# Two pads in SBUF that move u, w0, w1, h, k and t to multiples of 64 bytes

## The chip, the cores and the metric

The kernel runs on one core of a Trainium2 chip. The metric is the device time of one execution in microseconds, as the median of several runs. Beside the times there is one profiled execution, from whose trace all rows below come. A second core is not used, so there is no exchange between cores.

## The reference

For 4 batches, 12 heads, 448 tokens and head width 64, the reference computes attention in which the heads are mixed before and after the softmax, and then a feed-forward block:

```python
scores = scale * q @ k^T                        # per head, 448 x 448
scores = einsum('bhij,hg->bgij', scores, w_pre) # mix heads
attn = softmax(scores)
attn = einsum('bhij,hg->bgij', attn, w_post)    # mix heads again
x = (attn @ v), heads side by side              # 4 x 448 x 768
u = x + (x^T @ U @ V)^T                         # rank 32, along the tokens
out = u + relu(u @ w_ch1) @ w_ch2               # 768 -> 3072 -> 768
```

## The kernel before

**Attention.** The work is cut into 16 units of at most 120 tokens. For a unit, `qk` (L381) multiplies q by k in float32, two heads at a time, into PSUM; `qk_out` (L385) copies the scores to a buffer s; `relay` (L388) sends each head's rows of s by DMA into t, where the partitions hold (token, head) pairs. `premix` (L412) multiplies t by the mixing weights, `neg_max` (L417) and `exp` (L422) make the softmax, `postmix` (L447) mixes again and transposes, `post_out` (L455) copies to a buffer a, and `av` (L488, L496) multiplies by v and puts the result in `acc`. Every matmul of this part is in float32; a float32 matmul stands in the trace as two instructions. There are two t buffers, t0 and t1, three q, two k and three s.

**Rank-32 step.** For two of the 768/128 columns at a time, `flip` (L677) transposes acc, `by_u` (L694) multiplies the result (xh and xl, 256 columns wide) by U, and `by_v` (L708) multiplies a buffer t3 by the buffer v4 (448 columns). The last two run in float32r, as the feed-forward block does.

**Feed-forward block.** u and the weights are split in a high and a low float32r part, and each product is made as three matmuls. `up` (L750) streams uh or ul of a batch (128 x 448) past a 128 x 128 block of w0h or w0l: 18 matmuls for one block f of 128 hidden columns and one batch. `down` (L770) streams hh or hl past blocks of w1h or w1l. f runs over 24 blocks and b over 4 batches, so that there are 24 x 4 x 18 = 1,728 matmuls at L750 and as many at L770, 3,456 in all. `relu_h` (L755) and `relu_l` (L759) write hh and hl, `gather` (L773) adds the products to acc, and `store` (L776) writes acc out. Weights arrive in pieces as 64-bit words in a buffer kr (`piece`, L568 to L638). Each piece is narrowed by five steps on VectorE (L596, L600, L601, L605, L606), one on ScalarE (L589) and one on GpSimd (L610), through a pair of buffers x and a, and then written into w0 or w1 (L299, L306). Pieces take turns with their x and a: those of one piece are in the pool tmp1, those of the next in tmp2.

**Order.** A planner lays out the order of all steps from costs and ranks. From f = 2 on the order of the steps on each engine is written out by hand (`lines`, L823 to L846). Neither reads an address.

**Where the buffers lie.** SBUF is filled from two sides. Pools of the left side follow one another upwards from byte 1,152 of each partition, those of the right side downwards from byte 229,344. When a stage ends, its pools are given back and the feed-forward buffers take their place, all from the right. A buffer's size is rounded up to a multiple of 32 bytes. Counted from the sizes in the code, the first bytes before are these, and what remains after division by 64:

| buffer | first byte | remainder |
|---|---|---|
| kr (2) | 222,176 and 225,760 | 32 |
| tmp1 | 219,104 | 32 |
| tmp2 | 44,416 | 0 |
| k (2), later u of batch 0 | 197,600 and 208,352 | 32 |
| q (3) | 188,672, 191,648, 194,624 | 0, 32, 0 |
| s (3) | 177,920, 181,504, 185,088 | 0 |
| u of batch 1, 2, 3 | 176,096, 148,448, 80,864 | 32 |
| w0 (2) | 169,952 and 120,800 | 32 |
| w1 (3) | 102,368, 108,512, 114,656 | 32 |
| h (12 of 1,792 bytes) | from 126,944 | 32 |
| t0, t1 | 148,256, 126,752 | 32 |
| xh, xl, t3, u4, v4 | 47,488, 51,584, 55,680, 57,216, 59,264 | 0 |
| v, a1, a0, e (3) | 61,056, 73,344, 93,504, from 114,176 | 0 |

The rows inside these buffers are 1,792 bytes (k, t, u, h, s) or 3,072 bytes (w0, w1), multiples of 64, so that every row of a buffer has the remainder of its first byte. The rows of a are 480 bytes: even rows have remainder 0, odd rows 32. In `av` the two heads of a pair read an even and an odd row beside each other.

Of the kernel before, what the change touches and what calls it, by code (L numbers as in the profile page):

```python
# [8 lines left out]
F32 = mybir.dt.float32  # L9
F32R = mybir.dt.float32r  # L10
I32 = mybir.dt.int32
# [7 lines left out]
B, H, S, D = 4, 12, 448, 64  # L19
# [16 lines left out]
HW = DM // 2  # L36
# [45 lines left out]
def f32(ap):  # L82
    return ap.bitcast(F32)
# [159 lines left out]
def build(tc, q2, kt, vj, wpre_in, wpost_in, u_in, v_in, ident, w1j, w2, out, show=None):  # L243
    nc = tc.nc
    whole, tail_ctx, a_ctx, mix_ctx, t1_ctx, t0_ctx, qk_ctx = (ExitStack() for _ in range(7))
    sb = {}

    def pool(ctx, name, bufs, side="left", **kw):
        sb[name] = Pool(ctx.enter_context(tc.tile_pool(name=name, bufs=1, side=side, **kw)), plan.where)
        return sb[name]  # L250
# [17 lines left out]
    p = pool(whole, "c", 1)  # L268
# [6 lines left out]
    pool(mix_ctx, "wc", 1)  # L275
    for n in ("e", "wr", "st"):
        pool(mix_ctx, n, BUFS[n])
    pool(t1_ctx, "t1", 1)
    pool(t0_ctx, "t0", 1)
    for n in ("kr", "tmp1"):  # L280
        pool(whole, n, BUFS[n], "right")
    for n in ("k", "q", "s"):
# [7 lines left out]
    T = {}  # L290
# [166 lines left out]
    for k in range(NC // 2):  # L457
        r = 2 * k
        us = sorted({chunks[2 * k][0], chunks[2 * k + 1][0]})
        pre, post, st, e, wr = ("pre", k), ("post", k), ("st", k), ("e", k), ("wr", k)  # L460
# [107 lines left out]
    def piece(key, src, n, p, rank, finish, slots, opened, cost, early=None, steady=False):  # L568


        count[0] += 1
        which = f"tmp{1 + count[0] % 2}"

        def pair(slot):
            T["nx", key], T["na", key] = (sb[slot[0]].tile([128, HW], I32, e, slot) for e in "xa")

        def get():
            return T["raw", key][:p, :n], T["nx", key][:p, :n], T["na", key][:p, :n]

        def load_raw(eng):  # L580
            T["raw", key] = sb["kr"].tile([128, 2 * S], F32, "kr", raw)[:, :2 * HW].bitcast(I32).rearrange("p (n t) -> p n t", t=2)
            eng.dma_start(out=T["raw", key][:p, :n], in_=src)

        def narrow0(eng):
            pair(first_tmp)
            raw, x, a = get()
            top = raw[:, :, 1]
            if eng is nc.scalar:
                eng.activation(out=f32(x), in_=f32(top), func=ACTF.Abs)  # L589
            else:  # L590
                eng.tensor_scalar(out=x, in0=top, scalar1=0x7FFFFFFF, scalar2=None, op0=ALU.bitwise_and)

        def narrow1(eng):
            raw, x, a = get()
            top = raw[:, :, 1]
            eng.tensor_scalar(out=a, in0=top, scalar1=LOW_EXP, scalar2=3, op0=ALU.bitwise_and, op1=ALU.logical_shift_left)  # L596

        def narrow2(eng):
            raw, x, a = get()
            eng.scalar_tensor_tensor(out=a, in0=raw[:, :, 1], scalar=SIGN_TOP, in1=a, op0=ALU.bitwise_and, op1=ALU.bitwise_or)  # L600
            eng.scalar_tensor_tensor(out=f32(a), in0=f32(x), scalar=MIN_NORMAL, in1=f32(a), op0=ALU.is_ge, op1=ALU.mult)  # L601

        def narrow3(eng):
            raw, x, a = get()
            eng.tensor_scalar(out=x, in0=a, scalar1=SIGN_EXP, scalar2=None, op0=ALU.bitwise_and)  # L605
            eng.scalar_tensor_tensor(out=f32(x), in0=raw[:, :, 0].bitcast(U32), scalar=2.0**-52, in1=f32(x), op0=ALU.mult, op1=ALU.mult)  # L606

        def narrow4(eng):
            raw, x, a = get()
            eng.tensor_tensor(out=f32(a), in0=f32(a), in1=f32(x), op=ALU.add)  # L610

        def put(eng):
            T["nf", key] = dram.tile([128, HW], F32, "nf" + "_".join(str(k) for k in key))
            eng.dma_start(out=T["nf", key][:p, :n], in_=f32(get()[2]))

        def take(eng):
            pair(tmp)
            eng.dma_start(out=f32(get()[2]), in_=T["nf", key][:p, :n])

        s = n / HW  # L620
        raw, tmp = ("kr", key), (which, key)
        kept = early is not None and len(early) == 2
        first_tmp = ("tmp1", (key, "early")) if early else tmp
        r0 = early[1] if early else rank
        plan.add((key, 0), [("SP", (480, 1800 * s))], load_raw, r0 - RANK["raw"], [early[0] if early else opened], [raw])
        plan.add((key, "abs"), [("ACT", 60 + 395 * s), ("DVE", 60 + 210 * s)][:1 if steady else 2], narrow0, r0, [(key, 0)], [raw, first_tmp])
        plan.add((key, 1), [("DVE", 60 + 212 * s)], narrow1, r0, [(key, "abs")], [raw, first_tmp])
        plan.add((key, 2), [("DVE", 120 + 1000 * s)], narrow2, r0, [(key, 1)], [raw, first_tmp], port=("DVE",))
        plan.add((key, 3), [("DVE", 120 + 750 * s)], narrow3, r0, [(key, 2)], [raw, first_tmp], port=("DVE",))
        plan.add((key, 4), [("POOL", 100 + 900 * s), ("DVE", 60 + 410 * s)][:1 if steady else 2], narrow4, r0, [(key, 3)], [first_tmp], port=BOTH)  # L630
        if kept:
            plan.add((key, "put"), [("SP", (480, 900 * s))], put, r0, [(key, 4)], [first_tmp])
            plan.add((key, "take"), [("SP", (480, 900 * s))], take, rank - RANK["raw"], [(key, "put"), opened], [tmp])
        used = tmp if kept or not early else first_tmp
        if early and not kept:
            rank = r0
        plan.add((key, 5), cost[0], lambda eng: finish(0, eng, f32(get()[2])), rank, [(key, "take" if kept else 4), opened], [used] + slots, port=BOTH)
        plan.add((key, 6), cost[1], lambda eng: finish(1, eng, f32(get()[2])), rank, [(key, 5)], [used] + slots, port=BOTH)  # L638
# [153 lines left out]
    for f in range(KF):  # L792
# [8 lines left out]
        for b in range(B):  # L801
# [9 lines left out]
            n = 1 if (f, b) == (KF - 1, B - 1) else 2  # L811
# [20 lines left out]
    for f in range(RANK["even"], KF):  # L832
        for b in range(B):
            lines["PE"].append(("up", f, b))
            key = ("w", f + 1, b)
# [79 lines left out]
```

## Time and profile before

| | |
|---|---|
| median of 3 runs | 1097.73 us (1089.36 to 1101.10) |
| profiled execution | 1100.28 us |
| its span, first to last instruction | 1098.5 us |
| mean granted TensorE clock | 0.992 |
| TensorE matmul busy | 1059.1 us (96%) |
| VectorE, ScalarE, GpSimd busy | 666.5, 408.4, 271.9 us |

The profiled execution's own time is 1.8 us more than its span. Busy times are sums over the span; matmuls overlap in the records, so the pace of a run of matmuls is read from their starts or from the chain of waits, not from the duration of one. [...]

### The profile page before, as it was taken

The numbers are of one execution on the slowest core, as the hardware profiler recorded it, in microseconds if no ns is written. First come the engines' busy times: TensorE is split into PE (matmuls) and PEld (weight loads), VectorE is DVE, ScalarE is ACT, GpSimd is POOL, SyncE is SP. The second block draws the span as 40 slices with busy tenths as digits, with TensorE's granted clock in tenths as the row PEclk, the third lists the DMA queues.
The fourth block names the chain that finished last, engine by engine and source line by source line (L and its number), as shares of the span: only waits on it lengthen the run. The fifth ranks groups of instructions, "written<-read, shape, count | busy, mean of one in ns | idle before, by whom it ended". The sixth has DMA issues, their size and how long they took to land.

```text
span 1098.5 us, 28397 instructions
## 1 busy us (share of the span) xinstructions
PE 1059.1 (96%) x12120; PEld 874.2 (80%) x12120; DVE 666.5 (61%) x1076; ACT 408.4 (37%) x852; POOL 271.9 (25%) x398
## 2 busy tenths in 40 slices
PE   4798999999999999999999999999999999999998
PEld 1365666665666899999999999999999999999997
DVE  0574564565688687665665666565666566566634
ACT  2786677677768721222112212212221211221200
POOL 3131111111224522232222222222222222222200
PEclk8899999999999999999999999999999999999999
DMA  7665646635755211221122212111211211221105
GB/s 277 191 187 171 196 128 193 200 119 167 213 198 163 82 31 44 58 58 58 44 58 58 58 44 58 56 46 58 58 48 53 58 44 57 58 58 44 44 1 200
DMA packets 52270, 108.11 MB, mean 98 GB/s; under 512 B 5056, under 2 KB 38320, under 8 KB 51632
## 3 DMA queue, kind: packets, MB, share of 16 engines
q1 hardware_dynamic: 52144, 106.30, 31.4%
q8 instruction: 95, 1.56, 0.6%
q14 instruction: 31, 0.25, 0.1%
HBM read 57.91 MB, written 7.08 MB: 59 GB/s over the span
## 4 chain that ended last, share of the span: by engine, by line
PE 89%; DMA 4%; ACT 3%; DVE 2%; issue 2%; SPq 0%; POOL 0%; ACTq 0%; DVEq 0%
PE bank L750 33%; PE bank L770 33%; PE bank L447 6%; PE bank L488 5%; PE bank L381 5%; PE bank L412 5%; DMA t<-s 3%; ACT e L422 2%; PE bank L496 1%; DVE mx L417 1%; PE bank L677 1%; PE bank L694 1%; ACT s L299 1%; DMA k<-in_kt 0%; ACT a L299 0%
## 5 line engine op out<-in xcount | busy, mean ns | idle before, releaser
L773 DVE TENSOR_TENSOR acc<-acc,bank 128x896 f32<-128x896 f32 (+1 forms) x153 | 163.5, 1070 | 173.5 <-PE bank L770 172.9
L755 ACT ACTIVATE hh<-bank 128x448 fp32r<-128x448 f32 x96 | 52.4, 546 | 492.2 <-PE bank L750 312.2
L750 PE MATMUL bank<-uh,w0l 128*128 128x448 f32 x576 | 212.2, 368 | 0.0
L770 PE MATMUL bank<-hh,w1l 128*128 128x448 f32 x576 | 212.1, 368 | 0.0
L770 PE MATMUL bank<-hl,w1h 128*128 128x448 f32 x576 | 211.9, 368 | 0.0
L770 PE MATMUL bank<-hh,w1h 128*128 128x448 f32 x576 | 211.9, 368 | 0.0
L750 PE MATMUL bank<-uh,w0h 128*128 128x448 f32 x576 | 211.9, 368 | 0.0
L750 PE MATMUL bank<-ul,w0h 128*128 128x448 f32 x576 | 211.9, 368 | 0.0
L610 POOL TENSOR_TENSOR a<-a,x 128x384 f32<-128x384 f32 (+2 forms) x98 | 98.6, 1006 | 422.6 <-PE bank L750 381.2
L417 DVE TENSOR_REDUCE mx<-bank 128x2 f32<-128x896 f32 x90 | 97.7, 1088 | 69.5 <-PE bank L412 63.7
L447 PEld LDWEIGHTS bank<-wr,e 60*64 60x64 f32 x5040 | 89.4, 135 | 45.8 <-issue 31.9
L422 ACT ACTIVATE e<-bank,mx 128x448 f32<-128x448 f32 x180 | 113.3, 642 | 13.0 <-DVE mx L417 9.2
L770 PEld LDWEIGHTS bank<-hh,w1l 128*128 128x128 f32 x576 | 108.1, 188 | 11.1 <-DVE acc L773 0.3
L770 PEld LDWEIGHTS bank<-hh,w1h 128*128 128x128 f32 x576 | 108.1, 188 | 10.9
L750 PEld LDWEIGHTS bank<-uh,w0l 128*128 128x128 f32 x576 | 108.1, 188 | 10.9
L750 PEld LDWEIGHTS bank<-uh,w0h 128*128 128x128 f32 x576 | 108.1, 188 | 10.9
L770 PEld LDWEIGHTS bank<-hl,w1h 128*128 128x128 f32 x576 | 108.1, 188 | 10.8
L750 PEld LDWEIGHTS bank<-ul,w0h 128*128 128x128 f32 x576 | 108.1, 188 | 10.8
L381 PE MATMUL bank<-k,q 64*64 64x448 f32 (+1 forms) x768 | 96.1, 569 | 15.5 <-ACT s L299 9.0
L759 DVE SCALAR_TENSOR_TENSOR hl<-bank,hh 128x448 fp32r<-128x448 f32 x96 | 59.9, 624 | 81.3 <-ACT hh L755 81.3
L447 PE MATMUL bank<-wr,e 60*64 60x60 f32 x5040 | 93.3, 219 | 8.9 <-issue 6.6
L412 PE MATMUL bank<-t,wpre 64*64 64x448 f32 x720 | 87.6, 557 | 8.8 <-DMA t<-s 5.8
(61 smaller groups left out, 1105.1 us busy)
## 6 DMA issues: line engine op xcount, KB each, us to landing
t<-s SPq DMA_DIRECT2D x192, 210.0 KB
kr<-in_w1j SPq DMA_DIRECT2D x48, 384.0 KB
kr<-in_w SPq DMA_DIRECT2D x48, 384.0 KB
v<-in_vj SPq DMA_DIRECT2D x4, 1536.0 KB
q<-in_q SPq DMA_DIRECT2D x32, 186.0 KB
out<-acc SPq DMA_DIRECT2D x9, 448.0 KB
k<-in_kt SPq DMA_DIRECT2D x4, 672.0 KB
k<-in_kt SPq DMA_DIRECT2D x4, 448.0 KB
```

The costliest lines, as they stand in the source:

```text
L381: eng.matmul(o[at, i, :S], lhsT=q[d, p, at], rhs=k[d, p, :], start=True, stop=True)
L412: eng.matmul(o[64 * j:64 * j + 64, i, :S], lhsT=wpre[64 * i:min(64 * i + 64, QW)], rhs=tt[u % 2][64 * i:min(64 * i + 64, QW), n, :], start ...
L417: eng.tensor_reduce(out=mx, in_=T["pre", k][:, :, :S], axis=AX.X, op=ALU.max, negate=True)
L422: eng.activation(out=e[:, i], in_=T["pre", k][:, i, :S], func=ACTF.Exp, bias=T["mx", k][:, i:i + 1], accum_out=sm[:, i:i + 1])
L447: eng.matmul(d, lhsT=e[64 * j:64 * j + HALF, i, x * KB:x * KB + KB], rhs=wr[64 * j:64 * j + HALF, i].rearrange("p (g m) -> p g m", m=MH), ...
L488: eng.matmul(main[i * D:(i + 1) * D, c, :n], lhsT=v[:, p + c, i, x, :], rhs=a[:, x * H + 2 * (p + c) + i, :n], start=(c == 0 and x == 0), ...
L610: eng.tensor_tensor(out=f32(a), in0=f32(a), in1=f32(x), op=ALU.add)
L750: eng.matmul(ps, lhsT=w[:, c * 128:(c + 1) * 128], rhs=u[:, c, :], start=(i == 0), stop=(i == 3 * KC - 1))
L755: eng.activation(out=hh, in_=T["up", f, b], func=ACTF.Relu)
L759: eng.scalar_tensor_tensor(out=hl, in0=T.pop(("up", f, b)), scalar=0.0, in1=f32(T["hh", f, b]), op0=ALU.max, op1=ALU.subtract)
L770: eng.matmul(ps[:, j, :S], lhsT=w[:, (c + j) * 128:(c + j + 1) * 128], rhs=h, start=(i == 0), stop=(i == len(todo) - 1))
L773: eng.tensor_tensor(out=two(b, c, n), in0=two(b, c, n), in1=T.pop(("dn", f, b, c))[:, :n, :S], op=ALU.add)
```

## The change

Three lines differ. A tile of 32 bytes, `gap`, is put into the pool st, which lies just below t1 and t0; both move up by 32 bytes. A tile of 480 bytes, `pad`, is put at the very top of the right side. And the tile kr has 2 x 384 words instead of 2 x 448, of which 2 x 384 were used before as well; the two kr buffers take 1,024 bytes less. All other buffers of the right side move up by 1,024 - 480 = 544 bytes. Nothing reads or writes the two pads.

```diff
     for n in ("e", "wr", "st"):
         pool(mix_ctx, n, BUFS[n])
+    sb["st"].tile([128, 8], F32, "gap")
     pool(t1_ctx, "t1", 1)
     pool(t0_ctx, "t0", 1)
+    pool(whole, "pad", 1, "right").tile([128, 120], F32, "pad")
     for n in ("kr", "tmp1"):
         pool(whole, n, BUFS[n], "right")
...
-            T["raw", key] = sb["kr"].tile([128, 2 * S], F32, "kr", raw)[:, :2 * HW].bitcast(I32).rearrange("p (n t) -> p n t", t=2)
+            T["raw", key] = sb["kr"].tile([128, 2 * HW], F32, "kr", raw).bitcast(I32).rearrange("p (n t) -> p n t", t=2)
```

Counted in the same way, the first bytes after are: kr 222,720 and 225,792, tmp1 219,648, k and u of batch 0 198,144 and 208,896, u of the other batches 176,640, 148,992 and 81,408, w0 170,496 and 121,344, w1 from 102,912, h from 127,488, t0 148,288, t1 126,784, all with remainder 0; s from 178,464 with remainder 32, and q 189,216, 192,192 and 195,168 with remainders 32, 0 and 32. The buffers in the last two rows of the table above, tmp2 and acc stay where they are.

## Rows read from the trace of the kernel before

**Rows 1.** The page: busy time by engine, slices, and the chain that ended last.
```profile
PE 1059.1 (96%) x12120; PEld 874.2 (80%) x12120; DVE 666.5 (61%) x1076; ACT 408.4 (37%) x852; POOL 271.9 (25%) x398
...
PE   4798999999999999999999999999999999999998
...
PE 89%; DMA 4%; ACT 3%; DVE 2%; issue 2%; SPq 0%; POOL 0%; ACTq 0%; DVEq 0%
PE bank L750 33%; PE bank L770 33%; PE bank L447 6%; PE bank L488 5%; PE bank L381 5%; PE bank L412 5%; DMA t<-s 3%; ACT e L422 2%; PE bank L496 1%; DVE mx L417 1%; PE bank L677 1%; PE bank L694 1%; ACT s L299 1%; DMA k<-in_kt 0%; ACT a L29
```

**Rows 2.** Windows by stage: stretch, its length, busy time (count) by engine.
```profile
core 0: us, PE busy (x) PEld busy (x) DVE busy (x) ACT busy (x) POOL busy (x), PEclk, DMA share, GB/s
0.00:25.00 25.00, 11.00 (x72) 2.85 (x72) 0.00 (x0) 6.25 (x8) 9.28 (x6) 0.85 0.80 284
50.00:150.00 100.00, 93.63 (x2415) 61.19 (x2407) 59.73 (x100) 72.17 (x158) 18.97 (x59) 1.00 0.55 171
410.00:1090.00 680.00, 680.00 (x3292) 617.66 (x3291) 414.23 (x671) 133.73 (x264) 175.20 (x173) 1.00 0.19 55
1090.00:1099.00 9.00, 4.82 (x24) 4.04 (x22) 3.01 (x5) 0.00 (x0) 0.00 (x0) 1.00 0.48 181
```

**Rows 3.** The chain of waits, 405 to 415 us: start, length, piece.
```profile
405.26 0.95 PE bank L694 x8
406.22 2.47 PE bank L770 x12
408.69 0.41 PE bank L708 x2
409.11 4.96 PE bank L770 x24
```

**Rows 4.** Instructions of lines L750 and L708: count, shortest/median/longest in ns.
```profile
L750 PEld LDWEIGHTS bank<-uh,w0l x576: 186/188/190, 367.2 to 1072.8; 128*128 128x128 f32 x192
L750 PE MATMUL bank<-uh,w0l x576: 362/368/472, 367.2 to 1073.0; 128*128 128x448 f32 x192
...
L708 PEld LDWEIGHTS bank<-v,t x24: 186/189/192, 132.3 to 408.5; 128*128 128x128 f32 x24
L708 PE MATMUL bank<-v,t x24: 358/370/475, 132.3 to 408.7; 128*128 128x448 f32 x24
```

**Rows 5.** Timeline of TensorE from 396.5 us: one `up`, and the next instruction.
```profile
396.52 0.37 PE L750 MATMUL bank<-uh,w0l 128*128 128x448 f32 x1
...
400.18 0.27 PE L677 MATMUL bank<-ident,acc 128*112 128x128 f32 x1
```

**Rows 6.** Timeline of TensorE in attention, two stretches: start, length, instructions.
```profile
54.55 2.07 PE L488 MATMUL bank<-a,v 128*64 128x120 f32 x36
56.55 0.58 PE L496 MATMUL bank<-a,v 64*64 64x60 f32 x24
...
62.59 0.93 PE L412 MATMUL bank<-t,wpre 64*64 64x448 f32 x8
63.34 0.87 PE L447 MATMUL bank<-wr,e 60*64 60x60 f32 x48
```

**Rows 7.** Timeline of VectorE: two steps of two successive weight pieces.
```profile
605.21 0.56 DVE L600 SCALAR_TENSOR_TENSOR a<-kr,a 128x384 int32<-128x384 int32 x1
...
606.87 0.56 DVE L606 SCALAR_TENSOR_TENSOR x<-kr,x 128x384 f32<-128x384 uint32 x1
...
611.41 0.56 DVE L600 SCALAR_TENSOR_TENSOR a<-kr,a 128x384 int32<-128x384 int32 x1
...
613.43 0.56 DVE L606 SCALAR_TENSOR_TENSOR x<-kr,x 128x384 f32<-128x384 uint32 x1
```

**Rows 8.** The chain of waits at the start: start, length, piece.
```profile
2.53 4.45 DMA k<-in_kt
...
11.36 9.71 DMA t<-s
```

**Rows 9.** Waits of the DMA queue: who waited for whom, us in total, times, longest.
```profile
SPq L582 <- DVE x L606: 614.0, 86, 26.9
```

## The prediction

> **What bounds the kernel.** Read the page first. TensorE's matmuls are busy 96% of the span, and in the 40 slices only the first two fall under 9 tenths for more than a moment. The chain that ended last agrees: 89% of it is matmuls, 33% each at L750 and L770, the two halves of the feed-forward block, and 5% each at L381 and L412, which stream k and t. Only 4% is DMA, nearly all of it the relays t<-s, 3% [rows 1]. Then the windows by stage: from 410 to 1090 us matmuls are busy for 680.00 of 680 us at a granted clock of 1.00, while VectorE has 414 and ScalarE 134 us of work and the DMA engines are 19% busy [rows 2]. No transfer and no other engine can shorten this stretch; it is the number of matmuls times their pace. In the chain of waits 24 of them take 4.96 us, or 0.2067 us each [rows 3], and there are 3,456. Before 410 us the matmuls are still busy 94 of 100 us [rows 2], and before 50 us the chain goes through DMA [rows 8].
>
> **What the change is to the machine.** No instruction is added, removed or put in another place: the planner reads no address, and the pads are never touched. What changes is the first byte of some buffers. So the question for each user of a moved buffer is whether its time depends on a remainder of 0 or 32 bytes after division by 64. The kernel before answers it, since it has the same kinds of instructions on buffers of either remainder.
>
> **Feed-forward matmuls (u, w0, w1, h: 32 to 0).** They stream 448 float32r columns past 128 x 128 weights, all operands with remainder 32. The matmul at L708 has the same shape and type, its streamed operand v4 and its weights t3 have remainder 0, and it stands in the midst of the others. In the chain two of them take 0.41 us, 0.205 each, right before 24 of the others at 0.2067 [rows 3]. The difference of 1.7 ns is under what the rounding of 0.41 allows (2.5 ns each), and other rows point the other way: the median duration at L708 is 370 ns against 368 at L750 [rows 4], and one `up`, with remainder 32, goes 18 matmuls in 400.18 - 396.52 = 3.66 us, 0.2033 each [rows 5], faster than the two with remainder 0. The bounds: -1.7 ns x 3,456 = -5.9 us, and +2 ns x 3,456 = +6.9 us. I take 0, as the rows on both sides straddle it.
>
> A second look at the same thing. At L694 the operands also have remainder 0 (xh, xl, u4), with 256 columns, and eight take 0.95 us, 0.1188 each [rows 3]. From there to L708's 0.205 it is 0.0862 us for 192 columns, 0.449 ns a column. If a start in the middle of 64 bytes cost one fetch of 64 bytes more, that is 16 columns, it would cost 16 x 0.449 = 7.2 ns, and L750 and L770 would show 212 ns beside L708's 205. They show 206.7 and 203.3.
>
> Weight loads are 188 ns at L750 and 189 at L708 [rows 4], and they lie beside the matmul before: with 680 us of matmuls in 680 us [rows 2], a load that were some ns shorter would give nothing back. 0.
>
> [...]
>
> **Attention matmuls (k, t: 32 to 0).** They are float32. A `premix` is eight instructions, two rounds of four that run in the four 64 x 64 corners side by side, and takes 63.34 - 62.59 = 0.75 us: 0.375 for 448 columns of t, 0.837 ns a column, with remainder 32. In `av` 18 pairs of 120 columns take 56.55 - 54.55 = 2.00 us, 0.111 a pair, 0.93 ns a column, where one of each pair has remainder 0 and the other 32 [rows 6]. A stream that is wholly at 32 is not slower per column than a half-and-half one, whose ends weigh more. L381 and L412 are 10% of the chain [rows 1], 110 us; one fetch of 29 saved (1,792 bytes are 28 times 64, and touch 29 when they start in the middle) would be 3.8 us. Bounds -3.8 and 0; I take 0.
>
> **DMA (t, k, kr: 32 to 0; s, q the other way).** A relay reads rows of s and writes rows of t. Before, s is at 0 and t at 32; after, it is the reverse, since s moves by 544 bytes with the rest of the right side. If a row's cost went by the 64-byte pieces that it touches, one end would gain 1/29 and the other lose 1/28, of 3% of 1098.5 us, 33 us [rows 1]: -1.1 and +1.2 us. The first load of k is 4.45 us on the chain [rows 8], 1/29 of it 0.2 us. Weight pieces wait for VectorE to free kr, 614 us in all at L582 [rows 9], so their transfers are early already. Sum 0, bounds -1.3 and +1.2 us.
>
> **VectorE, ScalarE, GpSimd.** Successive weight pieces use tmp1 (32) and tmp2 (0). L600 takes 0.56 us for both, and so does L606 [rows 7]. These engines are also not what ends last after 410 us; the cover is the 680 us of matmuls over 414 of VectorE [rows 2]. 0. The copies into s, now at 32, are written by instructions that the same rows say don't mind. 0.
>
> **Handing over of buffers.** When stages end, the feed-forward buffers lie over given-back ones, and a shift could make one wait for another owner. By the addresses of both kernels one pairing is new (the high part of the third w1 over the second e) and some fall away (w0 over the second e, the third low part of w1 over the first). e is read last by the attention, long before the third w1 is written. No new wait; 0.
>
> **The sum** is 1100.28 + 0 = 1100.3 us for the profiled execution (span 1098.5 and 1.8 around it). That execution is 2.55 us above the median of the runs shown, 1097.73, so the forecast for a median is 1097.7. The bounds add to -11.0 (5.9 + 3.8 + 1.3) and +8.1 us (6.9 + 1.2): 1086.7 to 1105.8, which takes in the spread of the three runs, 1089.36 to 1101.10. A measurement of this kernel can tell about 1%, 11 us, from no change.
>
> **Rival 1, faster: the fetch of 64 bytes is real.** If each stream that starts in the middle of 64 bytes pays for one of 29 fetches, a feed-forward matmul gives back 206.7/29 = 7.1 ns, 24.6 us in all, and k and t 3.8: 1069.3 us. [...] Chance 0.09.
>
> **Rival 2, slower: s loses its place.** The relays read s at 32 instead of 0, and they are the one transfer on the chain. The pieces give +1.2 us, 1098.9; to make the kernel slower by 1%, 11 us, the 33 us of relays on the chain would have to grow by a third, to 1108.7 us. For it: in the first 25 us the DMA engines are 80% busy and the matmuls are not, a relay of 9.71 us is waited for [rows 2, 8]. Against it: the stores at the end read rows of acc, which start at any multiple of 8 bytes, and move 181 GB/s at a share of 0.48, 377 per full share, while the first 25 us have 284 at 0.80, 355 [rows 2]. Reads that start anywhere are no slower there. Chance 0.05.
>
> [...]
>
> **That the change doesn't do what it says** would mean that an address comes out otherwise, for instance that t stays at 32. By the rows above the time would be the same 1097.7, and it is in the forecast's chance.
>
> **How the numbers follow.** Forecast (no effect of the remainder) 0.86, rival 1 0.09, rival 2 0.05. The predicted time is 1097.7. The range is the forecast's own, 1086 to 1106; it leaves out both rivals, 0.14. Faster by over 1% is rival 1 and the very end of the forecast's bounds, 0.10; slower by over 1% is rival 2, 0.05; within 1% 0.85.
>
> **What would show it.** In the profile after, 24 matmuls at L770 in the chain between 410 and 1073 us should take 4.96 us again, and `premix` 0.75. If rival 1 holds, they take 4.79 (24 x 199.6 ns). If rival 2 does, the pieces DMA t<-s in the chain grow above 3% and the feed-forward block starts later than 367 us, with its pace unchanged. The forecast is wrong if a pace of matmuls moved by more than 2 ns either way; then the reading of L708 as a stand-in for L750 failed.

## The result, and the profile after

The kernel after takes 1100.72 us (median of 20 runs, 1095.33 to 1107.47), the kernel before, measured beside it, 1091.33 us (20 runs, 1083.35 to 1104.95). The ratio is 1.0098, 95% interval [1.0076, 1.012]: the change costs about 10 us. The ratio leaves out executions more than 1.5% above the fastest of their kernel, so it is not quite the quotient of the two medians. The time itself lies in the forecast's range, but its basis doesn't hold: the kernel before has a median of 1091, not 1098, and the change moved it, where no effect was forecast. The profiled execution of before, with 1100.28 us, is longer than 18 of those 20; that of after took 1099.74 us and is an ordinary one.

So the two profiles look alike, and that is the first thing to see. The page of after, busy time by engine and the chain by line (lines are two higher than before from `gap` and `pad` on):

```profile
PE 1058.6 (96%) x12120; PEld 874.3 (80%) x12120; DVE 666.7 (61%) x1076; ACT 407.7 (37%) x852; POOL 271.2 (25%) x398
...
PE bank L752 33%; PE bank L772 33%; PE bank L449 5%; PE bank L490 5%; PE bank L414 5%; PE bank L383 5%; DMA t<-s 4%; ACT e L424 2%; PE bank L498 1%; DVE mx L419 1%; ACT s L301 1%; PE bank L679 1%; PE bank L696 1%; DMA q<-in_q 1%; SPq L390 0%
```

Its windows by stage (the columns are those of [rows 2]):

```profile
50.00:150.00 100.00, 94.84 (x2432) 62.35 (x2433) 60.44 (x102) 73.32 (x161) 19.19 (x59) 1.00 0.55 173
...
410.00:1090.00 680.00, 680.00 (x3292) 617.56 (x3291) 414.19 (x671) 133.32 (x264) 174.96 (x173) 1.00 0.19 55
```

The same 3,292 matmuls in the same 680 us as in [rows 2]. The chain of waits of after, about 405 us and then about 613:

```profile
404.81 0.96 PE bank L696 x8
405.77 2.44 PE bank L772 x12
408.20 0.40 PE bank L710 x2
408.61 4.95 PE bank L772 x24
```

```profile
613.19 4.96 PE bank L772 x24
618.15 3.72 PE bank L752 x18
621.87 2.48 PE bank L772 x12
624.35 3.72 PE bank L752 x18
```

24 matmuls take 4.95 and 4.96 us, as in [rows 3]. The 12 ahead of the two at L710 take 2.44 us, 0.203 each, where [rows 3] have 2.47; this comes back below. By lines L752 and L710 (count, shortest/median/longest in ns), the answers to [rows 4]:

```profile
L752 PE MATMUL bank<-uh,w0l x576: 362/368/473, 366.8 to 1072.5; 128*128 128x448 f32 x192
...
L710 PE MATMUL bank<-v,t x24: 360/369/472, 131.7 to 408.2; 128*128 128x448 f32 x24
```

And `premix` in the timeline of TensorE takes 63.97 - 63.21 = 0.76 us, as 0.75 in [rows 6]:

```profile
63.21 0.93 PE L414 MATMUL bank<-t,wpre 64*64 64x448 f32 x8
63.97 1.10 PE L449 MATMUL bank<-wr,e 60*64 60x60 f32 x54
```

Nothing that lasts differs between these two executions. The 10 us must lie between after and an ordinary execution of before, of which there was no profile yet.

### The profile page after: what moved, and what is told of

The parts are those of the page before. It is cut to its first block, busy times and chain, and to the rows that moved or that the text cites. A ratio compares the mean times of both kernels' runs of the same rounds, so it can differ in the third digit from the quotient of the medians.

```text
span 1098.0 us, 28397 instructions
## 1 busy us (share of the span) xinstructions
PE 1058.6 (96%) x12120; PEld 874.3 (80%) x12120; DVE 666.7 (61%) x1076; ACT 407.7 (37%) x852; POOL 271.2 (25%) x398
## 4 chain that ended last, share of the span: by engine, by line
PE 88%; DMA 4%; ACT 3%; DVE 2%; issue 2%; SPq 1%; POOL 0%; ACTq 0%; DVEq 0%
PE bank L752 33%; PE bank L772 33%; PE bank L449 5%; PE bank L490 5%; PE bank L414 5%; PE bank L383 5%; DMA t<-s 4%; ACT e L424 2%; PE bank L498 1%; DVE mx L419 1%; ACT s L301 1%; PE bank L679 1%; PE bank L696 1%; DMA q<-in_q 1%; SPq L390 0%
## 5 line engine op out<-in xcount | busy, mean ns | idle before, releaser
L775 DVE TENSOR_TENSOR acc<-acc,bank 128x896 f32<-128x896 f32 (+1 forms) x153 | 163.5, 1070 | 173.6 <-PE bank L772 173.4
L752 PE MATMUL bank<-uh,w0l 128*128 128x448 f32 x576 | 212.2, 368 | 0.0
L752 PE MATMUL bank<-uh,w0h 128*128 128x448 f32 x576 | 211.9, 368 | 0.0
L752 PE MATMUL bank<-ul,w0h 128*128 128x448 f32 x576 | 211.9, 368 | 0.0
L752 PEld LDWEIGHTS bank<-uh,w0l 128*128 128x128 f32 x576 | 108.1, 188 | 10.9
L752 PEld LDWEIGHTS bank<-uh,w0h 128*128 128x128 f32 x576 | 108.1, 188 | 10.8
L752 PEld LDWEIGHTS bank<-ul,w0h 128*128 128x128 f32 x576 | 108.1, 188 | 10.8
```

What stands on the lines that cost most here:

```text
L752: eng.matmul(ps, lhsT=w[:, c * 128:(c + 1) * 128], rhs=u[:, c, :], start=(i == 0), stop=(i == 3 * KC - 1))
L775: eng.tensor_tensor(out=two(b, c, n), in0=two(b, c, n), in1=T.pop(("dn", f, b, c))[:, :n, :S], op=ALU.add)
```

## The experiments

All ratios below are against the kernel before, run beside on the same chip; the count is that of the runs. Line numbers differ from kernel to kernel with the lines put in; in the chains, pieces of 12, 24 and more at the higher of the two lines are `down`, pieces of 18 at the lower one `up`.

**Which of the moved buffers.** Four kernels: before once more; before with the gap alone; after without the gap; after with s put back.

```diff
e1: before, and
+    sb["st"].tile([128, 8], F32, "gap")
e2: after, and
-    sb["st"].tile([128, 8], F32, "gap")
e3: after, with the pools k, q, then a pool "spad" of one tile [128, 8], then s
```

> The kernel before, unchanged, measured against itself. Every theory: ratio 1.000 within its interval. It is here for a second profile of that kernel: the one on record took 1100.28 us, above its median of 1091.33. If the loss is in the feed-forward block, a profile near 1090 us shows 24 matmuls of that block in less than the 4.96 us that both profiles have; if it is in attention, that figure stays and the block begins some 8 us earlier than 367.2 us.

> The kernel before with the 32-byte gap alone: t0 and t1 at multiples of 64, everything else as before. If the place of t makes the loss (relays written at 0 instead of 32, or premix reading there): 1.010. If the place of s, or of u, w and h makes it: 1.000.

> The kernel after without the 32-byte gap: the right side is moved by 544 bytes (k, u, w0, w1, h, kr at multiples of 64, s at 32), t stays at 32. If s or the feed-forward operands make the loss: 1.010. If t makes it: 1.000. If only s and t together at opposite remainders matter, now both at 32: 1.000.

> The kernel after with 32 bytes more between q and s, so that s lies at multiples of 64 (and of 256) again, as before the change; all else as after. If the place of s makes the loss (rival 2 of the prediction): 1.000. If k, t or the feed-forward operands make it: 1.010.

Measured: e0 0.9987 [0.9966, 1.0009] (12 runs), e1 0.9991 [0.9963, 1.0019] (12), e2 1.0100 [1.0066, 1.0134] (6), e3 1.0107 [1.0075, 1.0139] (6). Neither t nor s has a part in it; rival 2 of the prediction is out. The loss comes with the move of the rest of the right side. The profiled execution of e0 took 1089.24 us, an ordinary one at last, and its chain of waits shows the 10 us:

```profile
408.51 2.44 PE bank L770 x12
410.96 0.41 PE bank L708 x2
411.37 4.87 PE bank L770 x24
...
612.01 4.86 PE bank L770 x24
616.88 3.65 PE bank L750 x18
620.53 2.43 PE bank L770 x12
622.96 3.65 PE bank L750 x18
```

The same 24 matmuls take 4.86 us instead of 4.96, and 18 of them 3.65 instead of 3.72. The last four pieces are 14.59 us for 72 matmuls, 0.2026 each; the same four pieces of after, shown above, are 14.88 us, 0.2067 each. The windows from 410 to 1070 us, before again and after, say the same with 3,258 matmuls and 3,196 in 660 us, at a granted clock of 1.00 in both:

```profile
410.00:1070.00 660.00, 660.00 (x3258) 611.58 (x3257) 409.00 (x665) 132.97 (x264) 175.54 (x173) 1.00 0.19 53
```

```profile
410.00:1070.00 660.00, 660.00 (x3196) 599.38 (x3195) 403.00 (x660) 132.78 (x263) 174.96 (x173) 1.00 0.18 51
```

Behind the last pair of `by_v` stand 3,318 of the 3,456 matmuls, and 4.0 ns each are 13.3 us. The spans of the two profiles differ by 1098.0 - 1087.5 = 10.5 us, and this long run begins at 408.61 us in after and at 411.37 in e0, which gives back 2.8: 13.3 - 2.8 = 10.5. The whole loss is this pace. The execution of before on record was at 206.7 ns as well, from 409 us to its end [rows 2, 3]. So before has both paces.

**Does the place set the pace, or is it kept from the start?** Theory 1: an unbroken run of matmuls keeps the pace that it falls into where it begins. Theory 2: operands at multiples of 64 have the slower pace for good. Two kernels get a matmul of another width into the stream now and then, and in two the operands are split up.

```diff
n1 (after) and n2 (before): in up, ahead of the loop over c,
+        if f > 2 and b == 0:
+            n = 264 + 8 * (f - 3)
+            eng.matmul(ps[:, :n], lhsT=wl[:, :128], rhs=uh[b][:, 0, :n], start=True, stop=True)
x3 (after): pads of 32 bytes ahead of w0_0, u2, w0_1 and u3, so that w0 and w1 have remainder 32 of 64, u and h 0
x4 (after): the same and one ahead of u0, so that u and h have 32, w0 and w1 0
```

> The kernel after with one matmul more ahead of up for batch 0 of each f from 3 to 23: 264 columns at f=3, 8 more at each next f, into the part of PSUM that the next matmul overwrites. 21 matmuls, 0.12 to 0.2 us each, some 3.5 us more work. Theory 1 (two paces, 206.7 and 202.7 ns, either of which an unbroken run of matmuls keeps from the moment it begins; the place of the operands only decides which one it falls into there): the pace changes at some of these matmuls and stays between them, so that stretches of 144 matmuls take 29.2 us in some and 29.8 in others. Theory 2 (with operands at multiples of 64 the lasting pace is 206.7, the faster one is a passing state after a break): 206.7 in all stretches, save for some matmuls after each break.

> The kernel before with the same 21 matmuls. Theory 1: stretches of both paces here too, and the mix need not be that of the kernel after. Theory 2: 202.7 ns throughout, or throughout as the execution began, since operands at 32 have the faster pace as their lasting one.

> The kernel after with w0 and w1 alone back at remainder 32 (pads of 32 bytes around them), u and h stay at 0. If the place of the stationary operands decides the pace of the last unbroken run: 1.000 against the kernel before, its matmuls at 202.7 ns. If that of the streamed ones decides: 1.010 and 206.7 ns.

> The kernel after with u and h alone back at remainder 32, w0 and w1 stay at 0. If the place of the streamed operands decides: 1.000 and 202.7 ns. If that of the stationary ones decides: 1.010 and 206.7 ns. If both must match, one of this pair and the one before it is fast, or neither is.

In n1, the kernel after, the chain of waits from 716 us (L751 is the matmul put in, L755 and L775 are `up` and `down`):

```profile
716.90 4.86 PE bank L775 x24
721.76 0.15 PE bank L751
721.92 3.71 PE bank L755 x18
725.63 2.48 PE bank L775 x12
...
746.71 4.96 PE bank L775 x24
751.67 0.16 PE bank L751
751.83 3.65 PE bank L755 x18
755.48 2.43 PE bank L775 x12
```

In n2, the kernel before (L749 is the one put in):

```profile
477.86 4.86 PE bank L773 x24
482.73 0.13 PE bank L749
482.85 3.71 PE bank L753 x18
...
507.64 4.96 PE bank L773 x24
512.60 0.13 PE bank L749
512.73 3.65 PE bank L753 x18
516.38 2.44 PE bank L773 x12
```

Both kernels go from either pace to the other at one matmul, and stay there until the next one is put in, 144 matmuls on. Theory 2 is wrong, with operands at either remainder, and Theory 1 holds: neither remainder has a pace of its own. (One run each: 1097.51 and 1095.92 us, a mixture as the chains show.) Not every matmul put in changes the pace: of the 21, 9 do in n1 and 12 in n2, and the same width need not do the same. The ones of 272 and 288 columns leave n1 at the better pace and take n2 from it to the slower one.

x3 gave 1.0061 [1.0035, 1.0087] and x4 1.0071 [1.0041, 1.0101] (10 runs each), neither of the two that any theory had. The chain of x3 shows why (L759 and L779 are `up` and `down`):

```profile
438.14 4.81 PE bank L779 x24
442.95 3.67 PE bank L759 x18
446.62 2.47 PE bank L779 x12
449.09 3.62 PE bank L759 x18
452.72 4.95 PE bank L779 x24
457.67 3.70 PE bank L759 x18
```

In x3, with the streamed operands at remainder 0 and the stationary ones at 32, the pace no longer stays: it goes up and down without any break, between 0.200 (4.81/24) and 0.206 us (4.95/24). x4, split the other way round, also lies between 1.000 and 1.010. The place of both operands counts here, then, and each on its own is no answer.

**One matmul to put it right.** If the run only needs another beginning, a single matmul ahead of it should give the kernel after the better pace.

```diff
z1 (after) and z2 (before): by_v counts its calls; in up, ahead of the loop over c,
+        if T.get("by_v") == B * KC // 2:
+            T["by_v"] = 0
+            eng.matmul(ps[:, :264], lhsT=wl[:, :128], rhs=uh[b][:, 0, :264], start=True, stop=True)
```

> The kernel after with a single matmul more, 264 columns (0.12 us), ahead of the first up that follows the last by_v, into PSUM that the next matmul overwrites. In the nudged kernels this width led to 202.7 ns from either pace. Theory 1: some 3,260 matmuls at 202.7 instead of 206.7 ns, 13 us less than the kernel after, so 0.998 to 1.001 against the kernel before. Theory 2 (206.7 is the lasting pace at multiples of 64): 1.010.

> The kernel before with the same single matmul. Theory 1: nothing in the executions that were fast already, 13 us less in the one in eight or so that was at 206.7 ns; 0.998 to 1.000, and fewer runs above 1095 us. Theory 2: 1.000.

Measured: z1 0.9990 [0.9967, 1.0013] (6 runs, 1085.33 to 1088.41), z2 1.0140 [1.0109, 1.0171] (6 runs). One matmul of 0.12 us takes the whole loss from the kernel after, and gives it to the kernel before. Both then keep the pace that they have behind it, as Theory 1 says. But z2 missed what was expected of it, 0.998 to 1.000: that 264 columns lead to the better pace from anywhere, as I had read from n1 and n2, is not so. The chain of z1, then that of z2, with L752 and L750 the matmul put in:

```profile
407.24 4.95 PE bank L776 x24
412.18 0.12 PE bank L752
412.31 12.77 PE bank L756 x63
```

```profile
415.34 4.87 PE bank L774 x24
420.21 0.12 PE bank L750
...
605.08 4.96 PE bank L774 x24
```

12.77/63 is 0.2027. In z2 the run begins at 4.87 and has 4.96 after it.

**What the beginning depends on.** The last break ahead of the long run is a pair of `by_v` matmuls at about 408 us, of which v4 and t3 are the operands. The change altered how u, w0, w1 and h lie to these. x5 gives the buffers of the rank-32 step (xh, xl, t3, u4, v4, and ident between them) the same distance as before the change; x6 puts the right side back to a remainder of 32.

```diff
x5: after, and ahead of the pool xn, then behind the pool c (ident, u4, v4)
+    pool(whole, "pad_xn", 1).tile([128, 8], F32, "pad_xn")
+    pool(whole, "pad_c", 1).tile([128, 8], F32, "pad_c")
x6: after, and
-    pool(whole, "pad", 1, "right").tile([128, 120], F32, "pad")
+    pool(whole, "pad", 1, "right").tile([128, 112], F32, "pad")
```

> The kernel after with the buffers of the rank-32 step (xh, xl, t3, u4, v4) moved to remainder 32, so that they stand to u, w0, w1 and h as before the change: 32 bytes apart within 64. If the last run of matmuls gets its pace from how its operands lie beside those of the by_v ahead of it: 202.7 ns and 1.000 against before. If from the operands' own remainder of 0: 206.7 ns and 1.010.

> The kernel after with a pad of 448 bytes instead of 480: the whole right side 32 bytes higher, u, w0, w1, h, k and kr at remainder 32 of 64 again (s at 0), though at other addresses than before (remainder 32 of 256 instead of 224), with the smaller kr and with t at 0. If the remainder of 64 is what the change's loss hangs on: 202.7 ns and 1.000. If it is the smaller kr, the distance of the move or what the buffers lie over: 1.010.

Measured: x5 0.9962 [0.9935, 0.9989] (4 runs), x6 1.0108 [1.0080, 1.0135] (4 runs). x5 has u, w0, w1, h, k and t at multiples of 64, as the change wanted, and the better pace; x6 has u, w0, w1, h and k at remainder 32 again and the worse one. The remainder of 64 is not what counts. Chain of x5, then of x6:

```profile
406.74 4.87 PE bank L775 x24
...
607.38 4.86 PE bank L775 x24
```

```profile
612.86 4.96 PE bank L772 x24
```

**The distance.** Theory 3: the distance modulo 128 between the feed-forward operands and those of the rank-32 step decides. Theory 4: any odd multiple of 32 bytes will do. The buffers of the rank-32 step are moved up by 96 or 64 bytes in three kernels. Those that lie above them on the left side, v, a, e and t among them, move too, by 64 or 128 bytes, here as in x5, and keep their remainder of 64.

```diff
x7 (after), x8 (before): ahead of xn, and 32 bytes behind v4 as in x5,
+    pool(whole, "pad_xn", 1).tile([128, 24], F32, "pad_xn")
x9 (x6): ahead of xn,
+    pool(whole, "pad_xn", 1).tile([128, 16], F32, "pad_xn")
```

> The kernel after with the buffers of the rank-32 step 96 bytes higher: the feed-forward operands then lie 32 bytes past them modulo 128 (0 in the kernel after, 96 in before and in the fast x5, 32 in the slow x6). Theory 3 (the distance modulo 128 between the operands of the last by_v and those of the run behind it decides the pace): as x6, 206.7 ns and 1.010. Theory 4 (any shift of the rank-32 buffers by an odd multiple of 32 bytes is enough, remainder 64): 202.7 ns and 0.997 to 1.000, as x5.

> The kernel before with the buffers of the rank-32 step 96 bytes higher, so that they and the feed-forward operands lie at the same remainder of 128, as in the kernel after; u, w0, w1, h, k, kr and t stay at remainder 32 of 64. Theory 3: 206.7 ns in the last run and 1.010, the loss of the change without the change. If u, w and h at a multiple of 64 are needed for the loss: 1.000.

> The slow x6 (pad of 448 bytes) with the buffers of the rank-32 step 64 bytes higher: distance modulo 128 is 96 again, as in before and x5. Theory 3: 202.7 ns and 0.996 to 1.000. If x6 was slow for its smaller kr or for where its right side lies: 1.010.

Measured: x7 1.0124 [1.0097, 1.0152], x8 0.9994 [0.9957, 1.0031], x9 0.9985 [0.9947, 1.0023] (10 runs each). Theory 4 falls with x7. x9 is as Theory 3 has it, but x8, with a distance of 0 modulo 128 as in after, keeps the better pace, so Theory 3 falls too. A longer modulus would fit both: modulo 256, after has 128 and x8 has 0. Theory 5 says 256, and two kernels test it without changing any remainder of 64 of the feed-forward operands.

```diff
y1 (after): ahead of xn,
+    pool(whole, "pad_xn", 1).tile([128, 32], F32, "pad_xn")
y2 (before): ahead of xn,
+    pool(whole, "pad_xn", 1).tile([128, 16], F32, "pad_xn")
```

> The kernel after with the buffers of the rank-32 step 128 bytes higher. Everything that the change put at a multiple of 64 stays there, and so do these buffers; only the distance modulo 256 becomes 0, as in the fast x8, instead of 128. Theory 5 (the distance modulo 256 decides): 202.7 ns and 0.997 to 1.001. Theory 3 (modulo 128, which x8 spoke against): 206.7 ns and 1.010. A remainder of 64: 1.010.

> The kernel before with the buffers of the rank-32 step 64 bytes higher. All remainders of 64 are those of the kernel before; the distance modulo 256 becomes 32, as in the slow x7, instead of 96. Theories 3 and 5: 206.7 ns and 1.012. A remainder of 64: 202.7 ns and 1.000.

Measured: y1 1.0010 [0.9977, 1.0043] (10 runs), y2 1.0133 [1.0087, 1.0179] (4 runs). In the chain of y1, then of y2:

```profile
612.99 4.86 PE bank L774 x24
```

```profile
611.09 4.96 PE bank L772 x24
```

The kernel after loses its loss when buffers that the change did not move are put 128 bytes higher, and the kernel before takes it on when they go up by 64. That the rank-32 buffers count and not v, a, e or t above them is seen from x7 and y1: both are the kernel after with those at the same places, 128 bytes up, and only the rank-32 buffers differ, 96 or 128 bytes up. One has the slower pace, the other the better one. All kernels with equal remainders of u, h, w0 and w1 and no matmul put in:

| kernel | rank-32 buffers, mod 256 | u, h, w0, w1, mod 256 | distance | ratio | last five pieces |
|---|---|---|---|---|---|
| before again, e1 | 128 | 224 | 96 | 0.9987, 0.9991 | b s s b b |
| x5 | 160 | 0 | 96 | 0.9962 | b s s b b |
| x9 | 192 | 32 | 96 | 0.9985 | b s s b b |
| before, execution on record | 128 | 224 | 96 | (1100.28 us) | s b b s s |
| x8 | 224 | 224 | 0 | 0.9994 | b s b b b |
| y1 | 0 | 0 | 0 | 1.0010 | b s b b b |
| after, e2 | 128 | 0 | 128 | 1.0098, 1.0100 | b b s b s |
| e3 | 128 | 0 | 128 | 1.0107 | s b s b s |
| x6 | 128 | 32 | 160 | 1.0108 | b b s b s |
| x7 | 224 | 0 | 32 | 1.0124 | b b b b s |
| y2 | 192 | 224 | 32 | 1.0133 | b b s b s |

The last column is read from the chain of each profiled execution. Its pieces are two `up` of 18 and three `down` of 18, 12 and 24 matmuls, at about 390 to 421 us; the last begins the long run. Between them stand, in turn, `by_u`, then `flip` and `by_v`, then `by_u`, then the last `by_v`. "b" is the better pace (3.64 to 3.66, 2.43 or 2.44, 4.86 or 4.87 us), "s" the slower one (3.71 or 3.72, 2.47, 4.94 to 4.96 us). So the loss can be seen to arise: every kernel but the execution on record comes to the last `by_v` at the better pace, and at distances 0 and 96 it is kept there, at 32, 128 and 160 it is lost. The execution on record came at the slower pace and kept that, which is how before comes to have both.

The pattern is the same in kernels at one distance that lie at different places, so it isn't a new chance with every move. How far the rule goes is less certain. Only y1 and y2 were forecast from a modulus of 256, a longer one was not tried, and x7 and y2 differ at one piece with the same distance: behind `flip`, which also reads acc, a buffer that stays in its place.

## Why the prediction was wrong

**What bounds the kernel** was read rightly: the number of matmuls times their pace, from 410 us on, and no transfer or other engine has a part in the result. t, s, the relays and the float32 matmuls were rightly costed at nothing: e1 is 0.9991, e3 no better than e2, and `premix` is 0.76 us. For the copies into s the prediction had only rows of other instructions [rows 7]; it is e3 that shows them to cost nothing.

**The step that failed** is the one on the feed-forward matmuls: "I take 0, as the rows on both sides straddle it". I had both paces in the rows, 0.2067 in the chain [rows 3] and 0.2033 over one `up` [rows 5], and took them for scatter around one price. They are two steady paces of the same instructions. 3,318 times the 4.0 ns between them is 13.3 us, more than either of my bounds of -5.9 and +6.9, which came from a piece of two matmuls and from medians of durations that overlap. The question that I put to the rows, whether a matmul at remainder 0 costs something else than one at 32, has the answer that I gave: at L708 and L750 there is no such price (0.205 us at remainder 0 beside 0.2033 and 0.2067 at 32 [rows 3, 5]), and x5 and y1 show the feed-forward operands at multiples of 64 without loss (0.9962 and 1.0010). The question was too narrow: what the address changes is which pace the whole run falls into where it begins, and I had no rival in which something is kept over 3,318 matmuls.

**The second failure** is the base. The sum went on the profiled execution, 1100.28 us, and on a median of 3 runs, 1097.73. Over 20 runs the median is 1091.33. That 1100.72 lies near the forecast of 1097.7 is luck: a base 6.4 us too high stood in for most of a loss of 9.4 us that was put at nothing. The sum of 1100.3 against 1099.74 of the profile after is luck of the same kind, since the profiled execution of before happened to be at the slower pace too. That the chain would show 4.96 us again came true and proved nothing.

**Rival 1** asked for 24 matmuls in 4.79 us; none of the kernels with operands at 0 has that throughout. **Rival 2** had the sign and the wrong mechanism: s back at its place (e3) leaves 1.0107. **The handing over of buffers** was right: in the long stretch the matmuls of after have no more waits than those of before, 680.00 of 680 us busy.

**What stays open.** Why there are two paces, and why the distance modulo 256 sorts them, no run here shows; nor which of the rank-32 buffers it is. The distances 64, 192 and 224 were not tried, nor was it tried to keep the operands' places and change only the order of work at the beginning, other than by the one matmul. That the kernel before now and then has the slower pace fits Theory 1: in the execution on record an `up` at 392.01 us takes 3.72 us, while the same `up` in e0, at 394.26 us, takes 3.65, behind 12 matmuls at L770 that take 2.63 us in the one and 2.61 in the other, both more than 12 times either pace. In both the seventh of the 12 starts 0.26 us behind the sixth (390.51 - 390.25 and 392.78 - 392.52), some 0.05 us late, and from there on the two go at different paces. That this short wait sets the pace is argued, not shown, and how many executions of before are at the slower one is not known: only the profiled ones show it.

**The fastest version.** x5 is the fastest that was run, 0.9962 [0.9935, 0.9989] against before, with four runs of 1082.99 to 1085.34 us. Its pace is that of e0, and x9, which has the same distance, is at 0.9985 with an interval that includes 1. So what it has over before may be chance, and that it beats before is not shown. Against after it is 1.3% less (0.9962/1.0098 = 0.987).

## What to carry to other kernels

Where a long unbroken run of equal instructions bounds a kernel, look at its pace to the last per cent, in several executions, before you forecast an edit that moves buffers: two executions of the kernel before, with the same code, differed here by a pace that was kept to the end (4.96 and 4.86 us for 24 matmuls). A change of addresses that costs a per cent need not do so by the alignment that it was made for (here 1.0098 in after, and 0.9962 in x5 at the same remainders of the moved feed-forward operands); move an unrelated buffer, or put one small matmul ahead of the run, and see whether the effect goes with it. And one profile beside a median of three is no base: ask whether the profiled execution is an ordinary one.

## What the runs showed of the hardware that I had not expected

The float32r matmuls of 128 x 448 with a weight load each went at 0.2067 us in after and at 0.2026 in e0, at a granted clock of 1.00 in both windows. In these two kernels, whose streamed and stationary operands have the same remainder of 64, either pace lasted over the 3,318 matmuls of the long run. One matmul of 264 to 424 columns in between changed it, in either direction, at 9 of 21 places in n1 and at 12 in n2. In x3, where the remainders of the two kinds of operands differ by 32, the pace moved between 0.200 and 0.206 us by itself. And in the kernels of the table above the pace of the long run went with how far its operands lie, modulo 256 bytes, from those of the `by_v` matmuls just ahead of it: a run that came to them at the better pace kept it at 0 and 96 (4.86 or 4.87 us for the first 24) and lost it at 32, 128 and 160 (4.94 to 4.96 us). One that came at the slower pace, at a distance of 96, kept that one (before, the execution on record, 4.96 us).
